# Zero matmuls in TensorE's ramp, two products on VectorE, GpSimd's share of e from unit 0 on, and another written-out order

## The chip, the cores and the metric

The kernel runs on one core of one Trainium2 chip. The metric is the device time of one execution in microseconds (us); five executions of the kernel before gave a median of 214.37 us (214.12 to 215.14). The engines are TensorE (PE, with its weight loads shown apart as PEld), VectorE (DVE), ScalarE (ACT), GpSimd (POOL) and SyncE (SP), whose queue issues nearly all DMAs.

## The reference

The input x and f_logit have 4 batches of 6336 tokens of 256 channels, in float32. A gated recurrence over the tokens is followed by a highway layer:

```python
sig = 1.0 / (1.0 + np.exp(-f_logit))
f = lower_bound + (1.0 - lower_bound) * sig
i = 1.0 - f
for t in range(S):
    h = f[:, t] * h + i[:, t] * x[:, t]
    y[:, t] = h
# then, on the y of all tokens
H = np.maximum(y @ w_h, 0.0)
T = 1.0 / (1.0 + np.exp(-(y @ w_t + b_t)))
out = T * H + (1.0 - T) * y
```

## The kernel before

The tokens are cut into 25 units. Units 0 to 23 are 1024 tokens of one batch each (8 blocks of 128), taken batch after batch, so a unit continues the recurrence of the unit four before it; unit 24 holds the last 192 tokens of all four batches, 8 blocks of 96. The first part of a unit's work (a "front") may be cut in pieces, by the table CUTS: unit 0 in 0a (blocks 0 and 1), 0b (2 and 3) and 0c (4 to 7), units 1, 2 and 24 in halves a and b. Fronts of other units are whole. The second part (a "back") is whole for units 0 to 23 and in halves for unit 24.

What is done with a piece, by the letters of the list PLAN (in what follows "S0c.1" is letter S for piece 0c, second channel half, and "Z0.1" the second half of letter Z of unit 0):

- L and X load f_logit and x (SP, line 106; five buffers each); Q loads the two weight matrices (line 125).
- U: u = sigmoid(-f_logit) on ACT (line 154). P: the product u*x, one instruction for every two blocks, on POOL (line 160, called from `gpsimd_mul`). Letter p is the same product on DVE (`vector_mul`, line 166), for those listed in EARLY; EARLY is empty.
- A: PE transposes u (line 198) and F: ACT makes f from it (line 205). B: PE transposes the product (line 215). S: DVE scans the recurrence from f and the transposed product (line 230).
- W: DVE prepares the weights (line 148), once.
- Z and G: PE multiplies y by the two weight matrices (line 245). T: ACT takes the sigmoid of Z (line 251). D: DVE makes d from y and G (line 256). E: DVE makes e = d*t (line 166). H: POOL makes the last 512 columns of e (line 160) where `shared(j)` is not 0, which is for units 3 to 23 here. O: PE adds y and e up, transposed back to tokens (lines 296 and 297), in two groups q of a back. C and V copy the result out of PSUM on ACT and DVE (line 303); V is there for the last three backs only. R stores it (SP, line 309).

PLAN is one string in which every letter is the next instruction group of its kind; the digit behind A, B, Z, G and O is the PSUM slot (0 to 2). Each engine works through its own letters strictly in this order (`pin`). So a wait at one letter holds up all later letters on the same engine. Slots for A and B (16-bit) and for Z, G and O (float32) are apart; a slot can be written again when its reader is done. When a POOL product or H follows DVE products or Es in the list, it also waits for those (`gpsimd_mul`, the list `port`).

Of the kernel before, what the change touches and what calls it, by code (L numbers as in the profile page):

```python
# [11 lines left out]
FP32 = mybir.dt.float32  # L12
BF16 = mybir.dt.bfloat16
# [6 lines left out]
def kernel(  # L20
# [16 lines left out]
    nc = tc.nc  # L37
    B, S, D = x.shape
    assert D == 256
    P = 128  # L40
    NH = D // P
    NB = 8
# [16 lines left out]
    fronts, backs = [], []  # L59
# [6 lines left out]

    LASTQ = 2

    EARLY = []

# [7 lines left out]
    singles = ctx.enter_context(tc.tile_pool(name="singles", bufs=1))  # L80
# [4 lines left out]
    def new(key, shape, dtype):  # L85
        return pools[key].tile([P, *shape], dtype, tag=key, name=key)

    def pin(ins):
        return tc.keep_in_program_order(ins)
# [12 lines left out]
    def load(i, name, src):  # L102
        u, j0, j1 = fronts[i]
        np_, j = units[u][0], run(fronts[i])
        t = fs[i][name] = new(name, [NB, D], FP32)
        pin(nc.sync.dma_start(t[:np_, :j1 - j0].rearrange("p (k j) d -> p k (j d)", j=j), tokens(src, u, j0, j1, j)))
# [6 lines left out]
    def shape(piece):  # L113

        u, j0, j1 = piece
        return units[u][0], j1 - j0

    lb = singles.tile([P, NH], FP32, name="lb")
    bt = singles.tile([P, NH], FP32, name="bt")
# [4 lines left out]
    def load_weights(k):  # L124
        pin(nc.sync.dma_start(w_raw[:, 1 - k], (moe_w_t, moe_w_h)[k].rearrange("(h p) o -> p h o", p=P)))
# [25 lines left out]
    def gate(i):  # L151
        np_, nb = shape(fronts[i])
        u = fs[i]["u"] = new("u", [NB, D], FP16)
        pin(nc.scalar.activation(u[:np_, :nb], fs[i]["lt"][:np_, :nb], AF.Sigmoid, scale=-1.0))  # L154
# [13 lines left out]
    def product(i, k, mul):  # L168
        np_, _ = shape(fronts[i])
        if "bv" not in fs[i]:  # L170
            fs[i]["bv"] = new("bv", [NB // 2, D, 2], BF16)
        mul(inner(fs[i]["bv"][:np_, k:k + 1])[:, 0], fs[i]["u"][:np_, 2 * k:2 * k + 2],
            fs[i]["xt"][:np_, 2 * k:2 * k + 2])

    def width(piece):
        np_, nb = shape(piece)
        return np_ * nb
# [5 lines left out]
    def psum(slot, shape, key, dtype):  # L183
        tag = ("one" if dtype in (FP16, BF16) else "two") + slot
        return ps1.tile([P, *shape], dtype, tag=tag, name=key)
# [73 lines left out]
    SHARE = 512  # L259

    def shared(j):

        return SHARE if width(backs[j]) == NB * P and j >= 3 else 0

    def e_cols(j, a, e):
        if "e" not in bs[j]:
# [3 lines left out]
    def e_dve(j):  # L270
        vector_mul(*e_cols(j, 0, width(backs[j]) - shared(j)))

    def e_pool(j):
        gpsimd_mul(*e_cols(j, width(backs[j]) - shared(j), width(backs[j])))
# [37 lines left out]
    def each(pieces, count):  # L312
        return [(i, k) for i, piece in enumerate(pieces) for k in range(count(piece))]

    def halves_of(pieces):
        return each(pieces, lambda p: len(halves(p)))
# [7 lines left out]
    kinds = {  # L324
        "L": (lambda i, _: load(i, "lt", f_logit), each(fronts, lambda p: 1)),
        "X": (lambda i, _: load(i, "xt", x), each(fronts, lambda p: 1)),
        "Q": (lambda i, k: load_weights(k), [(0, 0), (0, 1)]),
        "U": (lambda i, _: gate(i), each(fronts, lambda p: 1)),
        "P": (lambda i, k: product(i, k, gpsimd_mul), [p for p in products if p not in EARLY]),
        "p": (lambda i, k: product(i, k, vector_mul), [p for p in products if p in EARLY]),  # L330
        "A": (decay_pe, halves_of(fronts)),
        "F": (decay_act, each(fronts, lambda p: NH)),
# [6 lines left out]
        "D": (d_dve, each(backs, lambda p: NH)),  # L339
        "E": (lambda j, _: e_dve(j), each(backs, lambda p: 1)),  # L340
        "H": (lambda j, _: e_pool(j), [(j, 0) for j in range(len(backs)) if shared(j)]),
        "O": (o_pe, groups),
        "C": (lambda j, q: o_copy(j, q, nc.scalar.copy, 0, group(j, q)[2]), [p for p in groups if group(*p)[2]]),
# [3 lines left out]
    }  # L347

    PLAN = (
        "XLLLXXLXLQQUUA0A1PFFFUFUB0PSSB1A0FFPSSPB1A0XLLXLXXPFUFSSWWPB1A0G0Z1PFFUPSSDPXLLXLB0A1G2Z0PUTFFTPPB1S"  # L350
        "SDUSSEZ1A0G0G2A1DDPFTFFPPZ1A0B1O0O2PSSTFECCUB0Z1B1G0G2SDSDA0Z0TUFTPPPPPPA0G1B1FXLLLXRRXLXDESA0Z0Z2O1"
        "UFTCTB0G0A1O1O2SDPPPFCCB1A0Z1G0O2FTUCB0G1PPPHPSDSEDPA1Z0Z2B0O1FTUCTESA1G0G1B0DDHPPPPSZ2O0O1FUTCCB1SA"
        "0G2Z0B1FDUTPHPPSXXLRLRRRLRXLRRZ1A0G2O0PDTFCEEG1B1A0O2O0UFCCDSG1B0A1Z2Z0SDPHPPPPFTTA1B0O2O1G0HPSFCCZ2"
        "B1A0Z1DUTFTEG0O2PSPLXXRXRRRRDPPHCB1SA0O1G0Z2B1FCUTDEPSG1Z0A0O2FTCPDPPHB1A0Z1G0O2SFTCDEB0Z1A1G0PLLXRR"
        "RRSDPPPUFTO2B0A1Z0G1SHDCFTEO2B0G0Z1A1PPPPCUFTSDHO2B0A1G0Z1SCFTO2B0A1DEPSZ1G0PPPCUFTDHO2B0A1O0G1SCFCD"
        "EZ2B0A1Z0PSTFTPPPG1B1O2A0O0DUCFCSG1Z2A1B0HDELXLLRXRLLRXRRRRRXPSTFPPZ1G0O2B1DTCSZ1G2A0O0PHUFTCDEB1A0G"
        "2Z1O0PSPFTCDPPHB0G1G2A1Z0UFTSA0B1FDEDSPO1O0Z2B0PPCCTPHSO1A1G0Z2B0UFTCDEPSA1G0Z2O1PPDB0FTCSA1Z2G0O1PH"
        "FUCTDELXRRXXRRLRLXXRRRA1B0G0Z1PSFTO2DCB1A0G1Z0O2PPPHSUFCTDEB1A0Z1G2O0PSDFTCB0A1Z1G2SFPPPHDO0B1A0G2ET"
        "UCFPSO1PZ0CDTB1A0Z1G2SFTUHO0A0B1DFG1EPPPPSO2A0CCZ0DFB1O2Z1B0TCUTSESHPPG0A1Z2G1DDRRRRRRRRFFTA1B0O2Z0Z"
        "1FCFSEHTTG2B1G0O1RSDDCO2SRHCZ0G1STRO2TDDEZ0CTERTG1O2O0DVDVCO2CREVO1CRO0RCVRR"  # L360
    )
    assert all(PLAN.count(k) == len(places) for k, (_, places) in kinds.items())
    todo = {k: iter(places) for k, (_, places) in kinds.items()}
    letters = iter(PLAN)
    for k in letters:
        kinds[k][0](*next(todo[k]), *([next(letters)] if k in "ABZGO" else []))
# [1 line left out]
_INS = ['x', 'f_logit', 'lower_bound', 'moe_w_h', 'moe_w_t', 'moe_b_t']  # L368
# [26 lines left out]
```

## Time and profile before

| what | us |
|---|---|
| median of five executions | 214.37 |
| the profiled execution, whole | 214.27 |
| its span, first to last instruction | 212.5 |
| busy DVE / ACT / PE / POOL | 195.4 / 193.7 / 186.1 / 161.1 |
| first S (scan) starts | 9.53 |
| last V and last C end | 207.24, 207.38 |
| last store's issue ends | 208.45 |

The profile is read in this manner: a group is one line of the kernel, with the engine, what it writes and reads, the number of instructions, their busy time and the mean time of one. "Idle before" is the time in which the engine stood still ahead of these instructions, and who ended it. Instructions on one engine overlap a little, so the distance from start to start is shorter than the time of one: for ACT 1.80 us for U of a whole unit, 1.00 for an F or T of 1024 columns and 0.90 for a C; for DVE 2.26 for a scan of 1024 columns, 1.17 for a D, 0.58 for an E of 1024 elements.

### The profile page before, as it was taken

To read this page: it belongs to the slowest core of one execution; us is meant where nothing else is said; L and a number is where in the kernel's file an instruction comes from. 1 tells how busy PE (TensorE), PEld (TensorE's weight loads), DVE (VectorE), ACT (ScalarE), POOL (GpSimd) and SP (SyncE) were. 2 spreads that over 40 slices of the span, in tenths; PEclk is the share of its full clock that TensorE was granted. 3 is DMA by queue.
4 is the path that set the end of the run, shared out by engine and by line. 5 is a ranking of instruction groups with operands and counts; after the bars stand their busy time and mean duration, and the time that the engine had idled before them with its cause. 6 is when DMAs were issued, how large, how long until landed. Compare 5 with 4: busy or idle time off the path is not lost.

```text
span 212.5 us, 4591 instructions
## 1 busy us (share of the span) xinstructions
PE 186.1 (88%) x1775; PEld 131.5 (62%) x1800; DVE 195.4 (92%) x154; ACT 193.7 (91%) x194; POOL 161.1 (76%) x133
## 2 busy tenths in 40 slices
PE   0368988799898999999999999999999899999980
PEld 0255655567565767666767766668576676866770
DVE  1269999999999999999999999999999999999980
ACT  2757999999999999999999999999999999998750
POOL 4485745979599698978988998898898876866500
PEclk9999999999999999999999999999999999999996
DMA  4999999999999999999999999999999996252466
GB/s 97 401 410 430 424 427 427 424 419 426 425 419 426 420 423 421 425 430 410 427 418 423 432 423 418 426 413 431 416 428 405 352 405 266 86 214 99 195 250 201
DMA packets 17350, 78.69 MB, mean 370 GB/s; under 512 B 2352, under 2 KB 2864, under 8 KB 11952
## 3 DMA queue, kind: packets, MB, share of 16 engines
q1 hardware_dynamic: 16784, 78.39, 90.3%
q8 instruction: 14, 0.23, 0.4%
q10 hardware_dynamic: 544, 0.00, 0.1%
q14 instruction: 8, 0.07, 0.1%
HBM read 52.43 MB, written 25.95 MB: 369 GB/s over the span
## 4 chain that ended last, share of the span: by engine, by line
DMA 35%; PE 26%; ACT 19%; DVE 8%; issue 7%; POOL 1%; SPq 1%; ACTq 1%; DVEq 0%; POOLq 0%
DMA xt<-in_x_dram 12%; DMA lt<-in_f_logit_dram 12%; DMA out_dram<-o 12%; PE zp L245 7%; PE gp L245 6%; ACT t L251 5%; ACT o L303 5%; ACT u L154 5%; ACT f L205 5%; DVE d L256 4%; PE op L296 4%; PE op L297 3%; PE uT L198 3%; PE bT L215 3%; DVE y L230 3%
## 5 line engine op out<-in xcount | busy, mean ns | idle before, releaser
L160 POOL TENSOR_TENSOR bv<-u,xt 128x512 bf16<-128x512 f16 (+1 forms) x100 | 114.7, 1179 | 31.5 <-DVE e L166 11.0
L230 DVE TENSOR_TENSOR_SCAN y<-f,y,bT 128x1024 bf16<-128x1024 f16 (+3 forms) x56 | 106.4, 1918 | 2.3 <-PE bT L215 2.3
L205 ACT ACTIVATE f<-uT,ncc 128x1024 f16<-128x1024 f16 (+3 forms) x60 | 66.0, 1111 | 2.5 <-PE uT L198 2.5
L251 ACT ACTIVATE t<-zp,bt 128x1024 bf16<-128x1024 f32 (+1 forms) x52 | 63.8, 1249 | 0.7 <-PE zp L245 0.3
L256 DVE SCALAR_TENSOR_TENSOR d<-y,ncc,gp 128x1024 bf16<-128x1024 bf16 (+1 forms) x52 | 62.3, 1208 | 0.3 <-issue 0.2
L245 PEld LDWEIGHTS <-w_sb 128*128 128x128 f16 x400 | 38.0, 99 | 37.7 <-issue 5.9
L303 ACT COPY o<-op 128x1024 f32<-128x1024 f32 (+2 forms) x50 | 55.7, 1159 | 4.2 <-PE op L297 2.1
L154 ACT ACTIVATE u<-lt 128x2048 f16<-128x2048 f32 (+3 forms) x30 | 53.3, 1780 | 5.2 <-DMA lt<-in_f_logit_dram 5.2
L245 PE MATMUL gp<-y,w_sb 128*128 128x512 bf16 (+1 forms) x187 | 50.6, 382 | 1.6 <-ACT t L251 0.4
L245 PE MATMUL zp<-y,w_sb 128*128 128x512 bf16 (+1 forms) x188 | 49.6, 378 | 1.7 <-DVE d L256 0.6
L296 PE MATMUL op<-diag,y 128*128 128x128 f16 (+1 forms) x400 | 49.2, 219 | 1.9 <-ACT t L251 0.7
L160 POOL TENSOR_TENSOR e<-d,t 128x1024 bf16<-128x1024 bf16 x21 | 44.9, 2136 | 7.4 <-DVE e L166 2.6
L297 PE MATMUL op<-ident_b,e 128*128 128x128 bf16 (+1 forms) x400 | 49.2, 219 | 0.0
L297 PEld LDWEIGHTS <-e 128*128 128x128 bf16 (+1 forms) x400 | 44.7, 114 | 5.6 <-issue 3.4
L296 PEld LDWEIGHTS <-y 128*128 128x128 bf16 (+1 forms) x400 | 44.8, 114 | 2.7
L198 PE MATMUL uT<-ident_h,u 128*128 128x128 f16 (+1 forms) x400 | 32.1, 226 | 10.2 <-ACT u L154 7.4
L198 PEld LDWEIGHTS <-u 128*128 128x128 f16 (+1 forms) x400 | 27.3, 101 | 17.4 <-ACT u L154 7.6
L215 PE MATMUL bT<-ident_f,bv 128*128 128x128 f32 (+1 forms) x200 | 32.3, 284 | 5.0 <-DVE y L230 2.4
L215 PEld LDWEIGHTS bT<-ident_f,bv 128*128 128x128 f32 (+1 forms) x200 | 22.8, 145 | 11.5 <-issue 4.6
L166 DVE TENSOR_TENSOR e<-d,t 128x1024 bf16<-128x1024 bf16 (+2 forms) x26 | 18.9, 734 | 0.1
L230 DVE TENSOR_TENSOR_SCAN y<-f,bT 128x512 bf16<-128x512 f16 (+2 forms) x8 | 10.5, 1337 | 4.0 <-PE bT L215 4.0
L135 DVE TENSOR_SCALAR cc<-lb 128x2 f32<-128x2 f32 x1 | 0.2, 169 | 4.5 <-DMA lb<-in_lower_bound_dram 4.5
(19 smaller groups left out, 10.9 us busy)
## 6 DMA issues: line engine op xcount, KB each, us to landing
out_dram<-o SPq DMA_DIRECT2D x48, 512.0 KB, 13.6
lt<-in_f_logit_dram SPq DMA_DIRECT2D x21, 1024.0 KB, 14.7
xt<-in_x_dram SPq DMA_DIRECT2D x21, 1024.0 KB, 15.5
lt<-in_f_logit_dram SPq DMA_DIRECT2D x5, 512.0 KB, 8.1
xt<-in_x_dram SPq DMA_DIRECT2D x5, 512.0 KB, 8.2
lt<-in_f_logit_dram SPq DMA_DIRECT2D x2, 384.0 KB, 13.2
xt<-in_x_dram SPq DMA_DIRECT2D x2, 384.0 KB, 11.7
xt<-in_x_dram SPq DMA_DIRECT2D x2, 256.0 KB, 5.1
```

The lines of the kernel that those rows point to most:

```text
L154: pin(nc.scalar.activation(u[:np_, :nb], fs[i]["lt"][:np_, :nb], AF.Sigmoid, scale=-1.0))
L160: ins = pin(nc.gpsimd.tensor_mul(out_, a, b))
L198: pin(nc.tensor.transpose(uT[:, j * np_:(j + 1) * np_], fs[i]["u"][:np_, j, h * P:(h + 1) * P], ident_h[:np_, :np_]))
L205: pin(nc.scalar.activation(f[:, :N].rearrange("p (k q j) -> p k q j", q=np_, j=j), fs[i]["uT", h].rearrange("p (k j q) -> p k q j", q=np_, ...
L215: pin(nc.tensor.transpose(t[:, k // r, k % r], fs[i]["bv"][:np_, k, h * P:(h + 1) * P].rearrange("p d j -> p (d j)").bitcast(FP32), ident_ ...
L230: pin(nc.vector.tensor_tensor_scan(y, fs[i]["f", h][:, c:c + w], fs[i]["bT", h][:, c:c + w], 0.0 if prev is None else prev, op0=ALU.mult, ...
L245: pin(nc.tensor.matmul(p[:, a:e], w_sb[:, k, ki, h * P:(h + 1) * P], y_of(j)[:, ki, a:e], start=ki == 0, stop=ki == NH - 1))
L251: pin(nc.scalar.activation(bs[j]["t"][:, m, :width(backs[j])], bs[j]["zp", m], AF.Sigmoid, bias=bt[:, m:m + 1]))
L256: pin(nc.vector.scalar_tensor_tensor(bs[j]["d"][:, m, :width(backs[j])], y_of(j)[:, m], ncc[:, m:m + 1], bs[j]["gp", m], op0=ALU.mult, op1 ...
L296: pin(nc.tensor.matmul(o, y[:, h, cols], diag[:, h], start=True, stop=False))
L297: pin(nc.tensor.matmul(o, bs[j]["e"][:, h, cols], ident_b, start=False, stop=True))
L303: pin(copy(bs[j]["o", q][:np_, a:e], bs[j]["op", q][:np_, a:e]))
```

## The change

Four things are edited. EARLY names two products, (0, 0) and (2, 0): the product of piece 0a and the first of piece 0c are now letter p, on DVE. `shared` no longer asks for j >= 3, so units 0, 1 and 2 have an H on POOL too, and their E on DVE is 1024 elements long where it was 2048. A tile of zeros, `filler`, is set by DVE, and a new letter M is one matmul of it, 128x128 by 512 columns, into a PSUM tile `busy` that nobody reads; `busy` has the float32 slot 2, whose next user is Z0.0. And PLAN is another string, with 21 Ms in it.

```diff
-    EARLY = []
+    EARLY = [(0, 0), (2, 0)]
...
+    filler = singles.tile([P, 512], BF16, name="filler")
+    nc.vector.memset(filler, 0.0)
...
-        return SHARE if width(backs[j]) == NB * P and j >= 3 else 0
+        return SHARE if width(backs[j]) == NB * P else 0
...
-        "XLLLXXLXLQQUUA0A1PFFFUFUB0PSSB1A0FFPSSPB1A0XLLXLXXPFUFSSWWPB1A0G0Z1PFFUPSSDPXLLXLB0A1G2Z0PUTFFTPPB1S"
-        "SDUSSEZ1A0G0G2A1DDPFTFFPPZ1A0B1O0O2PSSTFECCUB0Z1B1G0G2SDSDA0Z0TUFTPPPPPPA0G1B1FXLLLXRRXLXDESA0Z0Z2O1"
...
-        "1FCFSEHTTG2B1G0O1RSDDCO2SRHCZ0G1STRO2TDDEZ0CTERTG1O2O0DVDVCO2CREVO1CRO0RCVRR"
+        "LLXXLXQQUUMMMMMMMMMA0pFFMMMMB1PSLXLXLXLSA0MMMMB1UFFpSSWWMMA0PFFUXLXLMMB1PSA0PSUFFUPPG0G1Z2B1DDSZ0STT"
+        "A0B1PPHEFFUPSXXLA0SPFFUO1B0O2LLXXA1PSSPCCFFUPG0G1B0PPPDSSDZ2Z0A1A0TTFFEZ2B1Z1A0TTUFG0G2SDDB1HPPPPHPO"
...
+        "DHFFO2G1B1TCPSRO0A0O2PCCFDSERG1G0RDSHZ2Z1B1DFTTSZ2G0O1HTTSDDCO2G1EERDO0CDO2CVRO1RCVZ0RCVTRTEO2O1CVRR"
...
+    busy = psum("2", [NB * P], "busy", FP32)
...
+        if k == "M":
+            pin(nc.tensor.matmul(busy[:, :512], filler[:, :P], filler, start=True, stop=True))
+            continue
```

Read by engine, the start of the two lists is this:

| engine | before | after |
|---|---|---|
| SP | X0a L0a L0b L0c X0b X0c L1a X1a L1b Q Q X1b L2a L2b X2a L3 X2b X3 | L0a L0b X0a X0b L0c X0c Q Q L1a X1a L1b X1b L2a X2a L2b X2b L3 X3 |
| PE | A0a A0b B0a B0b A0c B0c A1a B1a A1b G0.0 Z0.0 B1b A2a G0.1 Z0.1 B2a Z1.0 A2b | M x9, A0a, M x4, B0a A0b, M x4, B0b, M x2, A0c, M x2, B0c A1a G0.0 G0.1 Z0.0 B1a Z0.1 A1b B1b A2a O0.0 B2a O0.1 A2b |
| DVE | S0a S0b S0c W W S1a D0.0 S1b D0.1 S2a E0 D1.0 D1.1 S2b E1 S3.0 | p0a S0a p0c S0b W W S0c D0.0 D0.1 S1a E0 S1b S2a D1.0 S2b D1.1 E1 S3.0 |
| ACT | ... U2a U2b T0.0 F2a F2a T0.1 U3 F2b.0 T1.0 F2b.1 F3.0 T1.1 F3.1 C0 C0 U4 | ... U2a T0.0 T0.1 F1b F1b U2b F2a F2a U3 C0 C0 F2b F2b U4 T1.0 T1.1 F3.0 F3.1 |

The end of the two lists on PE and DVE, from G23.0 and D23.0 on:

| engine | before | after |
|---|---|---|
| PE | G23.0 B24b G23.1 O21.1 O22.0 Z24a G24a O22.1 Z24b G24b O23.0 O23.1 O24a O24b.0 O24b.1 | G23.0 G23.1 Z23.0 Z23.1 B24b Z24a G24a O22.0 O22.1 G24b O23.0 O23.1 O24a Z24b O24b.0 O24b.1 |
| DVE | D23.0 D23.1 S24b D24a D24a E23 E24a D24b.0 V23.0 D24b.1 V23.1 E24b V24a V24b | D23.0 S24a.1 D23.1 S24b D24a D24a E23 E24a D24b.0 D24b.1 V23.0 V23.1 V24a E24b V24b |

More of the change, by code (lines that the diff above doesn't have):

```diff
@@ L349 @@
     PLAN = (
-        "XLLLXXLXLQQUUA0A1PFFFUFUB0PSSB1A0FFPSSPB1A0XLLXLXXPFUFSSWWPB1A0G0Z1PFFUPSSDPXLLXLB0A1G2Z0PUTFFTPPB1S"
-        "SDUSSEZ1A0G0G2A1DDPFTFFPPZ1A0B1O0O2PSSTFECCUB0Z1B1G0G2SDSDA0Z0TUFTPPPPPPA0G1B1FXLLLXRRXLXDESA0Z0Z2O1"
-        "UFTCTB0G0A1O1O2SDPPPFCCB1A0Z1G0O2FTUCB0G1PPPHPSDSEDPA1Z0Z2B0O1FTUCTESA1G0G1B0DDHPPPPSZ2O0O1FUTCCB1SA"
-        "0G2Z0B1FDUTPHPPSXXLRLRRRLRXLRRZ1A0G2O0PDTFCEEG1B1A0O2O0UFCCDSG1B0A1Z2Z0SDPHPPPPFTTA1B0O2O1G0HPSFCCZ2"
-        "B1A0Z1DUTFTEG0O2PSPLXXRXRRRRDPPHCB1SA0O1G0Z2B1FCUTDEPSG1Z0A0O2FTCPDPPHB1A0Z1G0O2SFTCDEB0Z1A1G0PLLXRR"
@@ L355 @@
[L355 to L359, printed above, removed]
@@ L360 @@
-        "1FCFSEHTTG2B1G0O1RSDDCO2SRHCZ0G1STRO2TDDEZ0CTERTG1O2O0DVDVCO2CREVO1CRO0RCVRR"
+        "LLXXLXQQUUMMMMMMMMMA0pFFMMMMB1PSLXLXLXLSA0MMMMB1UFFpSSWWMMA0PFFUXLXLMMB1PSA0PSUFFUPPG0G1Z2B1DDSZ0STT"
+        "A0B1PPHEFFUPSXXLA0SPFFUO1B0O2LLXXA1PSSPCCFFUPG0G1B0PPPDSSDZ2Z0A1A0TTFFEZ2B1Z1A0TTUFG0G2SDDB1HPPPPHPO"
+        "1O0B0UCCSSZ2A1G1Z0B0EDTFTPPSPPPA1O2G1O0DHFUCCB1A0G1Z2Z0SFTTA1B0DEPSLLLXXRXRRLXRRRFUPG2O1B1O0A0DPPHCC"
+        "G2FSDZ1Z0A1B0G2EPSTTFUPO1O0B1DPPHCCA0G2Z1SFDZ0A1B0EPSTFTUPG2O1A1B0O0DPPHCCG2Z1FSDA0B1Z0EPRRRRXLLSTFT"
@@ new lines @@
+        "PO2G1B0O0DPUCCESZ1G2A1Z0TFDB0A1G1PHPSDTFUO2B1O0CCPPPHSA0G1Z2Z0B1DFTEPSA0G1O2TPFDPPHB0O0G1A1UCCFSXLRX"
+        "RRLRRRLLRXXDZ2Z0B0A1EPSTTFPO1G2B1A0O0DPPHCUCFSG1Z2Z0B1A0DEPSTTFPG1O2B0O0A1DPPHUCFCSG1Z2DA1B0Z0EPSG1P"
+        "TFTDPPHB1O2O0G1A0UCCSZ2B1Z0FTDEPXRXRRRLRSTPA0O1G2O0B1DPPHFCCSA0G1Z2Z0B1DUFTEPSA0G1O2TPFCO0B0A1G2DPPH"
+        "CSFUDZ1Z0A1B0G2EPSTTFPLLRRXLXRRXRRDPPHO1O0B1A0CCSFUG1Z2Z0A0B1DTTFEPSPG1O2O0B1A0DPPHCCFUSZ2G1A0B1Z0DE"
+        "PSTTFPG1O2O0B1A0DPPHCCFUSG2Z1B0Z0A1RLRRRRXLRXXLLDEPSTFTPG2O1B1O0A0DPPHCUCFSG2Z1B1Z0A0DTTFEPSG2O1B1O0"
@@ L361 @@
+        "A0PDPPHCUCFSG2Z1B1Z0A0TFTDEPSPG2O1B0A1G0UCFDPPHSDO2Z1B1A0Z0TFTCPSPG1B0A1EZ0O2FTCUDSG1A1Z0B0RRRRRXRRE"
+        "DHFFO2G1B1TCPSRO0A0O2PCCFDSERG1G0RDSHZ2Z1B1DFTTSZ2G0O1HTTSDDCO2G1EERDO0CDO2CVRO1RCVZ0RCVTRTEO2O1CVRR"
     )
+    assert set(PLAN) <= {*kinds, *"M012"}
     assert all(PLAN.count(k) == len(places) for k, (_, places) in kinds.items())
     todo = {k: iter(places) for k, (_, places) in kinds.items()}
+    busy = psum("2", [NB * P], "busy", FP32)
     letters = iter(PLAN)
     for k in letters:
+        if k == "M":
+            pin(nc.tensor.matmul(busy[:, :512], filler[:, :P], filler, start=True, stop=True))
+            continue
```

## The prediction

> **What bounds the kernel now.** I read the page first, then busy time in 5 us stretches, then the start times of single instructions.
>
> ```profile
> PE 186.1 (88%) x1775; PEld 131.5 (62%) x1800; DVE 195.4 (92%) x154; ACT 193.7 (91%) x194; POOL 161.1 (76%) x133
> ...
> DVE  1269999999999999999999999999999999999980
> ACT  2757999999999999999999999999999999998750
> ```
>
> DVE and ACT are both full in the middle and idle only at the two ends. By stretches (columns: length, then busy us and instructions of PE, PEld, DVE, ACT, POOL, then granted clock, DMA share, GB/s):
>
> ```profile
> 10.00:15.00 5.00, 3.64 (x22) 2.78 (x22) 3.17 (x5) 2.63 (x5) 4.67 (x5) 1.00 1.04 410
> 15.00:20.00 5.00, 3.39 (x16) 2.31 (x17) 5.00 (x6) 3.62 (x6) 3.12 (x3) 1.00 1.04 428
> 20.00:25.00 5.00, 4.78 (x31) 2.93 (x31) 4.96 (x5) 4.66 (x6) 2.92 (x3) 1.00 1.02 427
> 25.00:30.00 5.00, 4.44 (x37) 2.48 (x37) 5.00 (x5) 5.00 (x6) 2.30 (x3) 1.00 1.00 423
> ```
>
> DVE is full from 14 us on, ACT from 25. From there ACT has no idle time until 188 us. A whole unit costs ACT 1.80 (U) + 2x1.00 (F) + 2x1.00 (T) + 2x0.90 (C) = 7.6 us, and DVE 2x2.26 + 2x1.17 + 0.58 = 7.44. So DVE's lead in work is no use where the f of the next scan is late, and here it is nearly late: F14.0 and its scan S14.0 start 1.40 us apart, of which F itself takes 1.31.
>
> ```profile
> 116.78 1.31 ACT L205 ACTIVATE f<-uT,ncc 128x1024 f16<-128x1024 f16 x1
> ...
> 118.18 2.34 DVE L230 TENSOR_TENSOR_SCAN y<-f,y,bT 128x1024 bf16<-128x1024 f16 x1
> ```
>
> **So the time is ACT's work, plus what ACT loses in the ramp, plus the tail behind the last scans.** The change does not alter ACT's work. I therefore ask when ACT ends U3 (27.06 us before; the letters that it has done by then are the same in both lists), and how long the tail is.
>
> **The clock.** The granted-clock column says 1.00 throughout the ramp, but durations say otherwise:
>
> ```profile
> 18.34 1.91 PE L245 MATMUL gp<-y,w_sb 128*128 128x512 bf16 x4
> ...
> 22.32 1.03 PE L245 MATMUL gp<-y,w_sb 128*128 128x512 bf16 x4
> ```
>
> The same four matmuls take 1.91 and 1.03 us (0.43 and 0.215 each): PE runs at half speed until about 21.1. The end shows what takes the clock away:
>
> ```profile
> 205.43:208.84 3.41, 1.08 (x19) 0.93 (x16) 1.37 (x2) 1.21 (x3) 0.00 (x0) 1.00 1.00 369
> 208.84:212.40 3.56, 0.00 (x0) 0.00 (x0) 0.00 (x0) 0.00 (x0) 0.00 (x0) 0.50 0.45 148
> ```
>
> It falls to 0.50 at 208.84, 2.3 us after the last matmul (206.5), with 1.08 us of PE work in the 3.4 us before.
>
> **The change, part by part.**
>
> *Edits at no cost.* The filler's memset meets a DVE that waits until 4.49; the first nine M (9x0.43 = 3.9 us from about 1.3) a PE that waits until 6.73 for U0a. Without that cover they would cost 0.3 and 3.9 us. Slot 2 has no other user before Z0.0. In work: DVE gains 3x0.53 on E0 to E2 (1.21 to 0.68) and pays two products. No DVE row shows a product of these types. [...] Above, 1.19, the row W: 512 elements, two float32 inputs from SBUF. [...] POOL pays 3x2.14 - 2x1.18 = 4.1 us; it is idle for 51 us.
>
> [...] No run here shows a product on DVE.
>
> *Loads.* Queue order sets landings: before, bytes land at some 512 KB in 1.25 us (423 GB/s), X0c at about 10.5, L1a at 11.7. With X0a third, it lands when the third 256 KB did (7.3, where U0b waited for L0b). X0c stays at 10.5; the two Q move ahead of L1a and make it 13.0. L3 moves from the place of 7168 KB to 7680 KB: 24.3 instead of about 23.2, before ACT asks for it. Stores move on SP too: R0.0 now stands behind X9, and lands near 60; C4.0, which needs its buffer, comes near 67. Hidden; without that cover, some 2 us.
>
> *The ramp's chain with PE at full speed.* p0a 7.3 to 8.0; B0a and S0a end at 9.9. p0c waits for X0c: 10.5 to 11.2. Behind it on DVE stand S0b and W, and on POOL the second product of 0c waits for it by `port`. S0b (1.3), W (2.3) and S0c (2.4) follow without a gap and end at 17.15, where before S0c ended at 16.46 and W at 18.68. G0.0 ends 0.5 us later, G0.1 and Z0.0 0.86 each, B1a 0.45, Z0.1 0.86: T0.1 starts at 20.9 (before 24.25, but with three Fs ahead of it). Then T 1.0, F1b 1.1, U2b 1.0, F2a 1.1 and U3 1.8 bring ACT to 26.9: **0.2 us ahead of before**. D0.0 comes at 17.8; counting DVE's letters on from there, S3.0 could start at 33.8 instead of 34.94. But ACT must now do C0 (1.8), U4 (1.8) and T1.1 (1.0) ahead of F3.0: 29.20 + 4.6 - 0.2 = 33.6, ended at 34.7, and B3.0 has F3.0's PSUM slot and comes after it: S3.0 at 35.2. F4.1 has 4.6 us more ahead of it (40.59 to 45.0), ending at 46.2; S4.1 started at 46.26. DVE's gain is gone by unit 4. Later, U23 and C18.1 stand ahead of F21.1 (171.27 + 2.7 - 0.2 = 173.8; with F's 1.45 there, S21.1 at 175.25 instead of 174.78). I take 0.3 us late into the tail, between -0.4 and +0.9.
>
> *Does the clock hold?* Between the last M (11.3) and the first G0.0 (15.8 half, 17.05 the rest) PE has B0c and A1a, 0.9 us in 4.5. That is less than the share with which it fell at 208.84. So I expect half speed again at G0.0. Before, the clock came 2.8 us after the first 512-wide matmul; 2.8 us at half speed lose 1.4 us, in just the chain to T0.1: **+1.4** (0 if the clock holds; 2.9 if it comes only behind Z0.1).
>
> [...]
>
> *The tail.* Before, Z24b stood ahead of O23.0. Now it stands behind O24a and waits for slot 0 besides (O23.0, read by V23.0). From the end of E23: three O at 0.89, Z24b 0.65 + 0.17 latency, two T 1.07, E24b 0.55, two half O 0.9 and V 0.69 with some 0.35 of hand-overs: 7.05 us. Before, E23's end at 201.84 to V's end at 207.24 are 5.4.
>
> ```profile
> 202.07 1.05 ACT L251 ACTIVATE t<-zp,bt 128x384 bf16<-128x384 f32 x2 [0.33 <-DVE e L166]
> ...
> 204.87 0.55 DVE L166 TENSOR_TENSOR e<-d,t 128x768 bf16<-128x768 bf16 x1
> ```
>
> The sigmoids that stood at 202.07, beside other work, now stand at the end of the chain. The last V comes 1.6 us later. Of that, 0.9 comes back: before, the last store queued 0.6 us behind two others, and now it has fewer bytes ahead. **+0.7** (0 to 1.5).
>
> **Sum.** 214.27 (the profiled execution, 0.1 under the median) + 0.3 + 1.4 + 0.7 = 216.7 us.
>
> **Rivals.**
>
> 1. *The clock holds* through the gap: 214.27 + 0.3 + 0.7 = 215.3 (214.3 to 216.2). For it: nine plus twelve Ms make PE denser than it ever was there. Against it: the row at 208.84.
> 2. *Faster: ACT is not what decides.* Place: F3.0 and F4.1. If T0.1 comes 1.5 us sooner than I count (ACT at U3's end 1.7 ahead), all of DVE's gain passes: 1.1 at S3.0 and 0.5 for E2, and the 0.42 us that DVE waited for a transpose at 76.4: 214.27 - 2.0 + 0.7 = 213.0; 212.6 with no loss in the tail. It decides when S4.1 starts below 45.5. For it: DVE has 10.3 us of idle time before 14 us, and the list for units 5 to 20 leaves F 0.5 us or more of room. Against it: ACT has no idle time to give between 25 and 188 us.
> 3. *Nothing is left over:* the front gains what the tail loses, 214.3; also what comes out if PE's clock does not matter to ACT at all.
>
> **Chances.** Forecast (clock falls back) 0.45; rival 1 0.17, of which 0.05 within 0.3%; rival 2 0.26; rival 3 0.12. A difference of 0.3% (0.64 us) is about what a measurement of this kernel can tell from none. So faster 0.26, same 0.17, slower 0.57. The range takes rival 2 down to 212.8 and the forecast with p at 1.19 and a later clock up to 218.2; some 2 in 10 lie outside. The forecast's own range is 215.3 to 218.2.
>
> **What would show it.** The G0.0 group of four 512-wide matmuls: 1.0 us if the clock holds, above 1.5 if it fell. T0.1's start: 20.9 or 22.3. U3's end: 26.9 or 28.3. S4.1 against 46.26. E23's end to the last V's end: 7.05 against 5.4. p's duration: 0.69 to 1.19. I am wrong if DVE's scans of units 3 and 4 do not wait for F, or if the last sigmoids are not on the chain.

## The result and the profile after

The changed kernel takes **214.87 us** (median of 24 executions, 214.66 to 216.19; the kernel before beside it 214.31): ratio **1.0029, 95% interval 1.0019 to 1.0038**. Slower, by 0.3% where 1.1% was forecast. The profiled execution took 214.82 us, its span is 213.0: 0.55 us over the 214.27 of before.

The page of the kernel after, as far as it answers to that of before:

```profile
PE 190.3 (89%) x1794; PEld 131.8 (62%) x1821; DVE 196.4 (92%) x157; ACT 194.4 (91%) x194; POOL 165.0 (77%) x134
...
DVE  2599796999999999999999999999999999999971
ACT  4569979999999999999999999999999999996851
```

DVE starts working earlier (2, 5 in its first two slices for 1, 2). But it now has holes, the 7 and the 6 in its fifth and seventh slices. The stretches show it in numbers (columns as before):

```profile
10.00:15.00 5.00, 3.14 (x26) 1.74 (x26) 5.00 (x7) 2.64 (x5) 2.37 (x3) 1.00 1.05 421
15.00:20.00 5.00, 3.89 (x26) 2.17 (x24) 4.53 (x5) 4.76 (x6) 4.58 (x5) 1.00 1.03 421
20.00:25.00 5.00, 2.73 (x35) 2.43 (x36) 4.07 (x4) 5.00 (x7) 5.00 (x4) 1.00 1.02 428
25.00:30.00 5.00, 4.95 (x44) 3.25 (x43) 4.86 (x5) 3.66 (x6) 3.36 (x4) 1.00 1.02 428
```

DVE is busy 5.00 of 5 us from 10 to 15 us (3.17 before), and loses 0.47 and 0.93 us in the next two stretches, where before it lost next to none (5.00 and 4.96).

**The clock held.** PE's four matmuls of a weight group take 1.03 us at 16.69, not 1.91:

```profile
15.62 1.24 PE L249 MATMUL gp<-y,w_sb 128*128 128x512 bf16 x5 [0.58 <-DVE y L234]
16.69 1.03 PE L249 MATMUL zp<-y,w_sb 128*128 128x512 bf16 x4
```

**Where the ramp's gain went.** DVE's timeline after, from the second early product to S3.0 (start, duration, and in brackets the idle time before with what ended it):

```profile
9.90 0.74 DVE L170 TENSOR_TENSOR bv<-u,xt 128x512 bf16<-128x512 f16 x1 [0.58 <-DMA xt<-in_x_dram]
...
11.81 1.39 DVE L152 SCALAR_TENSOR_TENSOR w_sb<-o,cc 128x512 f16<-128x512 f32 x2
...
16.03 2.47 DVE L260 SCALAR_TENSOR_TENSOR d<-y,ncc,gp 128x1024 bf16<-128x1024 bf16 x2 [0.47 <-PE gp L249]
...
20.66 0.96 DVE L170 TENSOR_TENSOR e<-d,t 128x1024 bf16<-128x1024 bf16 x1
...
25.14 2.33 DVE L234 TENSOR_TENSOR_SCAN y<-f,bT 128x512 bf16<-128x512 f16 x2 [1.08 <-PE bT L219]
...
33.83 1.39 DVE L170 TENSOR_TENSOR e<-d,t 128x1024 bf16<-128x1024 bf16 x1 [1.57 <-ACT t L255]
35.68 2.29 DVE L234 TENSOR_TENSOR_SCAN y<-f,bT 128x1024 bf16<-128x1024 f16 x1 [0.46 <-PE bT L219]
```

S2a waits 1.08 us because O0.0 stands ahead of B2a on PE and waits for H0 until 23.6. E1 waits 1.57 us for T1.1, which ACT does only after U4, and ACT stands idle ahead of U4 for its load:

```profile
27.25 1.28 ACT L209 ACTIVATE f<-uT,ncc 128x512 f16<-128x512 f16 x2
29.88 1.91 ACT L158 ACTIVATE u<-lt 128x2048 f16<-128x2048 f32 x1 [1.34 <-POOL bv L164]
31.69 2.10 ACT L255 ACTIVATE t<-zp,bt 128x1024 bf16<-128x1024 f32 x2
33.69 2.12 ACT L209 ACTIVATE f<-uT,ncc 128x1024 f16<-128x1024 f16 x2
```

The row names a GpSimd product, which ended at 29.81; the load itself landed at 29.79 (issued at 14.94, 14.85 us in the queue). U4 needs the load, not the product.

So the account from DVE's first scan to S3.0, by starts in the three profiles ("old list, filled" is the kernel before with nothing but the matmuls on zeros, run below):

| us | before | after | old list, filled |
|---|---|---|---|
| first scan starts | 9.53 | 8.05 | 9.06 |
| DVE idle from there to S3.0 | 1.83 | 4.16 | 1.39 |
| the two W | 2.30 | 1.39 | 1.39 |
| S3.0 starts | 34.94 | 35.68 | 33.07 |
| S4.1 starts | 46.26 | 46.94 | 44.74 |
| E23 starts | 201.26 | 201.79 | 199.98 |

After starts 1.48 us sooner and has 0.91 less of W, loses 2.33 more in waits and 0.62 in the second early product, which makes 0.56; it is 0.74 late at S3.0, the rest lying in small changes of length. From there to the tail DVE has no hole longer than 0.12 us, and the lateness is carried along: 0.68 at S4.1, 0.53 at E23.

**The tail.** DVE and ACT at the end, after:

```profile
207.16 0.56 DVE L170 TENSOR_TENSOR e<-d,t 128x768 bf16<-128x768 bf16 x1 [0.48 <-ACT t L255]
208.86 0.69 DVE L307 COPY o<-op 96x512 f32<-96x512 f32 x1 [1.13 <-PE op L301]
```

```profile
206.08 1.05 ACT L255 ACTIVATE t<-zp,bt 128x384 bf16<-128x384 f32 x2
```

The last sigmoids do stand on the chain (206.08, against 202.07 before), and E24b comes 2.3 us later. From E23's end to the last V's end it is 7.07 us, against 5.29. But from there to the span's end it is 3.50 us, against 5.25. The two differences cancel.

### The profile page after: what moved, and what is told of

Its sections match the earlier page's. It is cut to its first block, busy times and chain, and to the rows that moved or that the text cites. A ratio compares the mean times of both kernels' runs of the same rounds, so it can differ in the third digit from the quotient of the medians.

```text
span 213.0 us, 4618 instructions
## 1 busy us (share of the span) xinstructions
PE 190.3 (89%) x1794; PEld 131.8 (62%) x1821; DVE 196.4 (92%) x157; ACT 194.4 (91%) x194; POOL 165.0 (77%) x134
## 4 chain that ended last, share of the span: by engine, by line
PE 41%; ACT 28%; DMA 13%; DVE 10%; issue 5%; POOL 1%; SPq 1%; ACTq 0%; DVEq 0%; POOLq 0%
DMA lt<-in_f_logit_dram 11%; PE gp L249 10%; PE zp L249 9%; ACT f L209 9%; ACT t L255 8%; ACT u L158 7%; PE op L300 6%; PE op L301 6%; DVE y L234 5%; PE bT L219 5%; PE uT L202 5%; ACT o L307 4%; DVE d L260 3%; DMA xt<-in_x_dram 2%; POOL e L164 1%
## 5 line engine op out<-in xcount | busy, mean ns | idle before, releaser
L164 POOL TENSOR_TENSOR bv<-u,xt 128x512 bf16<-128x512 f16 (+1 forms) x98 | 112.1, 1176 | 26.9 <-DVE e L170 9.6
L209 ACT ACTIVATE f<-uT,ncc 128x1024 f16<-128x1024 f16 (+3 forms) x60 | 67.5, 1144 | 0.7 <-PE uT L202 0.7
L255 ACT ACTIVATE t<-zp,bt 128x1024 bf16<-128x1024 f32 (+1 forms) x52 | 61.3, 1279 | 1.3 <-PE zp L249 0.8
L164 POOL TENSOR_TENSOR e<-d,t 128x1024 bf16<-128x1024 bf16 x24 | 51.6, 2151 | 8.7 <-DVE e L170 7.4
L307 ACT COPY o<-op 128x1024 f32<-128x1024 f32 (+2 forms) x50 | 54.1, 1188 | 4.4 <-PE op L301 4.4
L249 PE MATMUL gp<-y,w_sb 128*128 128x512 bf16 (+1 forms) x177 | 48.0, 376 | 2.5 <-DVE y L234 0.9
L219 PE MATMUL bT<-ident_f,bv 128*128 128x128 f32 (+1 forms) x200 | 30.9, 276 | 6.0 <-DVE y L234 2.9
L202 PE MATMUL uT<-ident_h,u 128*128 128x128 f16 (+1 forms) x400 | 30.7, 219 | 2.6 <-ACT f L209 1.1
L170 DVE TENSOR_TENSOR e<-d,t 128x1024 bf16<-128x1024 bf16 (+1 forms) x26 | 18.8, 728 | 2.2 <-ACT t L255 2.1
L234 DVE TENSOR_TENSOR_SCAN y<-f,bT 128x512 bf16<-128x512 f16 (+2 forms) x8 | 10.5, 1342 | 2.1 <-PE bT L219 2.1
L373 PE MATMUL busy<-filler 128*128 128x512 bf16 x21 | 8.0, 531 | 1.2 <-DVE filler L120 1.2
```

The costliest lines, as they stand in the source:

```text
L164: ins = pin(nc.gpsimd.tensor_mul(out_, a, b))
L202: pin(nc.tensor.transpose(uT[:, j * np_:(j + 1) * np_], fs[i]["u"][:np_, j, h * P:(h + 1) * P], ident_h[:np_, :np_]))
L209: pin(nc.scalar.activation(f[:, :N].rearrange("p (k q j) -> p k q j", q=np_, j=j), fs[i]["uT", h].rearrange("p (k j q) -> p k q j", q=np_, ...
L219: pin(nc.tensor.transpose(t[:, k // r, k % r], fs[i]["bv"][:np_, k, h * P:(h + 1) * P].rearrange("p d j -> p (d j)").bitcast(FP32), ident_ ...
L234: pin(nc.vector.tensor_tensor_scan(y, fs[i]["f", h][:, c:c + w], fs[i]["bT", h][:, c:c + w], 0.0 if prev is None else prev, op0=ALU.mult, ...
L249: pin(nc.tensor.matmul(p[:, a:e], w_sb[:, k, ki, h * P:(h + 1) * P], y_of(j)[:, ki, a:e], start=ki == 0, stop=ki == NH - 1))
```

## The experiments

Each kernel was timed in five rounds beside the kernel before. All compute the reference's output in full. "To E23" is the start of E23 in the profile, less that of the kernel after (201.79).

| kernel | median us | range | ratio to before, interval | S4.1 less after's | to E23 |
|---|---|---|---|---|---|
| before | 214.31 | 213.69 to 215.32 | 1 | -0.68 | -0.53 |
| after | 214.87 | 214.66 to 216.19 | 1.0029 [1.0019, 1.0038] | 0 | 0 |
| no_fill | 215.42 | 214.69 to 216.30 | 1.0046 [1.0025, 1.0066] | +1.42 | +1.46 |
| no_share | 215.07 | 214.84 to 216.65 | 1.0046 [1.0021, 1.0072] | | |
| no_early | 214.96 | 214.84 to 215.50 | 1.0028 [1.0010, 1.0047] | +0.08 | +0.10 |
| l4_first | 215.72 | 215.52 to 216.41 | 1.0060 [1.0037, 1.0084] | +0.72 | +0.92 |
| old_tail | 214.95 | 214.77 to 216.26 | 1.0040 [1.0022, 1.0059] | -0.10 | -0.17 |
| t1_first | 216.58 | 215.16 to 218.15 | 1.0116 [1.0077, 1.0155] | +1.59 | +1.78 |
| t1_tail | 217.07 | 215.49 to 219.03 | 1.0115 [1.0077, 1.0153] | +2.29 | +2.50 |
| before_fill | 213.48 | 212.79 to 214.92 | 0.9962 [0.9941, 0.9984] | -2.20 | -1.81 |
| bf_share | 215.87 | 215.59 to 216.32 | 1.0069 [1.0046, 1.0092] | +0.26 | +0.81 |
| bf_share12 | 213.63 | 213.03 to 214.94 | 0.9971 [0.9949, 0.9993] | -2.13 | -1.53 |
| bf_fill2 | 213.10 | 212.84 to 213.77 | 0.9941 [0.9919, 0.9964] | -1.56 | -1.58 |
| bf_best | 213.39 | 213.04 to 214.55 | 0.9962 [0.9945, 0.9979] | -1.77 | -1.17 |

The last two columns say the same thing twelve times: what a kernel has lost or won by unit 4, it has lost or won, to within 0.6 us, at E23. They are of one profiled execution each, which need not be the median one: no_fill's took 216.30 us, before_fill's 213.00. The one profile of no_share is of an execution of 248.04 us and is not read.

### One part of the change undone

**no_fill**: the 21 Ms taken out of the new list.

```diff
-LLXXLXQQUUMMMMMMMMMA0pFFMMMMB1PSLXLXLXLSA0MMMMB1UFFpSSWWMMA0PFFUXLXLMMB1PS
+LLXXLXQQUUA0pFFB1PSLXLXLXLSA0B1UFFpSSWWA0PFFUXLXLB1PS
```

> The changed kernel without its 21 M. In its profile the clock rose at 7.0 us and T0.1 started at 19.4. Without M the clock should rise some 3 us behind the first G0.0 matmul (14.45), so T0.1 comes about 1.5 us later and U3 ends near 27 instead of 25.5. Theory 1 (ACT's order decides, and ACT then waits 1.34 us for the load L4 at 28.5 to 29.9): U4 absorbs nearly all of it, 214.9 to 215.3 us. Theory of the prediction (every us that ACT loses ahead of U3 comes out at the end): 216.2 to 216.5.

Measured: 215.42, 0.1 above the first range. The clock rises at 18.78 only, S3.0 is at 37.12 (35.68) in its profile, an execution of 216.30 us. By the medians the Ms are worth about half a microsecond in the new list, but the two intervals overlap, so this is not settled.

**no_share**: GpSimd's share of e from unit 3 on only, as before; the first three H leave the list.

```diff
-        return SHARE if width(backs[j]) == NB * P else 0
+        return SHARE if width(backs[j]) == NB * P and j >= 3 else 0
```

> The changed kernel with shared() asking for j >= 3 again and the first three H taken out of the list. In the changed kernel E0, E1, E2 (1024 elements) took 0.96, 1.39 and 1.14 us beside POOL's work, before (2048 elements) 1.20, 1.23 and 1.21; so DVE's work moves by 0.1 us only. Theory 1 (ACT's order decides): 214.7 to 215.0. Rival (GpSimd's share slows DVE where it matters, in the front): E0 to E2 cost the same but D, S and O of units 0 to 2 come earlier, 214.2 to 214.5.

Measured: 215.07. No gain and no clear loss: in the new list's order the share is not what costs.

**no_early**: no product on DVE.

```diff
-    EARLY = [(0, 0), (2, 0)]
+    EARLY = []
```

> The changed kernel with EARLY empty: both p are P on POOL, in the same places of the list. DVE has 1.46 us less work; the first scan comes some 0.8 us later (POOL takes 1.18 instead of 0.73), U3 ends up to 1 us later. Theory 1 (ACT's order decides, the wait for L4 absorbs it): 214.7 to 215.1. Rival (DVE's work decides, 1.07 us more of it in the changed kernel): 213.4 to 214.0.

Measured: 214.96, the same as with them. The two products bring the first scan forward (8.05 for 8.84) and bring the end nothing.

**old_tail**: the last forty letters in the old order.

```diff
-CO2G1EERDO0CDO2CVRO1RCVZ0RCVTRTEO2O1CVRR
+CO2Z1G0EERCTTDO2VDO1RVCO0CRREVCO2RO1CVRR
```

> The changed kernel with the last 40 letters in the order that the kernel before has: Z24b and G24b ahead of O23, T24b ahead of C23, V ahead of C. Theory 1 (the new order of the tail is neutral: in the changed kernel's profile E23's start to the end of the last V takes 7.76 against 5.98 us, but the last V to the span's end 3.45 against 5.27, because the stores no longer queue): last V about 1.8 earlier, the stores' queue back, time within 0.3 of 214.87. Theory 2 (the prediction's third step, which charged the tail with +0.7): 214.2.

Measured: 214.95; the last V ends at 207.99 (209.54 after) and the span is 213.0 in both. Theory 1 holds: no gain or loss by the tail's new order shows, and the prediction's third term was not there.

### Is it the load of unit 4?

**l4_first**: L4 and X3 change places in the load queue.

```diff
-FFUXLXLMMB1P
+FFUXLLXMMB1P
```

> The changed kernel with the loads L4 and X3 exchanged in SP's queue, nothing else. L4 lands some 2.5 us earlier, so ACT's 1.34 us of waiting ahead of U4 goes; X3 lands 2.5 us later, and POOL's products of unit 3 end near 34.5, about when B3.0 gets its PSUM slot from F3.0. Theory 1 (ACT's order decides): U4 to F3 come 1.3 us earlier, S4.1 near 45.7 instead of 46.94, and the end 0.5 to 1.0 us earlier, 213.9 to 214.4. Rival (DVE's own work decides from unit 5 on): S4.1 earlier but the end within 0.2 of 214.87.

Measured: 215.72, which neither theory had. U4 no longer waits for its load, but X3 comes later, and GpSimd stands idle 4.07 us for it. So H2 comes later and still runs when E2 starts, and E2 takes 2.11 us, where it took 1.14 in the kernel after:

```profile
30.08 7.23 POOL L164 TENSOR_TENSOR bv<-u,xt 128x512 bf16<-128x512 f16 x6 [4.07 <-DMA xt<-in_x_dram]
...
43.87 2.13 POOL L164 TENSOR_TENSOR e<-d,t 128x1024 bf16<-128x1024 bf16 x1
```

```profile
44.43 2.11 DVE L170 TENSOR_TENSOR e<-d,t 128x1024 bf16<-128x1024 bf16 x1
```

The DMA engines are full here (share 1.02 to 1.05 in the stretches above), and the wait moved from one load to the other: the products of unit 3 start at 30.08, in the kernel after at 27.52. In this profile the clock was at 0.50 from 23.50 to 26.91 as well, which in the kernel after it was not, and S2a waited 2.13 us for 1.08. That fall alone does not explain the time: 3.41 us at 0.50 take 0.008 off the mean granted clock of an execution, and the one with 0.994 took 215.52 us.

**t1_first**: U4 and the first two products of unit 4 behind T1.0, T1.1 and F3.0. **t1_tail**: that and old_tail's end.

```diff
-PCCFFUPG0G1B0PPPDSSDZ2Z0A1A0TTFFE
+PCCFFPG0G1B0PDSSDZ2Z0A1A0TTFUPPFE
```

> The changed kernel with the letters of U4 and of its first two products moved behind T1.0, T1.1 and F3.0, so that ScalarE does not stand idle 1.34 us at U4 for the load of unit 4 while T1 is ready. Theory 1 (VectorE's place at unit 4 is what the end inherits, and U4's wait for its load is what made E1 late): Z1.0 ends near 29.4, so T1.1 ends near 31.7 instead of 33.8, E1 starts at 32.3 instead of 33.8, S3.0 at 33.0 to 34.2 (35.7), S4.1 at 45.3 to 45.8 (46.9), and the time falls by 1.1 to 1.6, to 213.3 to 213.8. Theory 2 (ScalarE's total work, not this wait, sets S4.1, as the prediction has it): ScalarE loses the 1.34 us no less, because it waits for something else; S4.1 within 0.4 of 46.9 and 214.6 to 215.1.

> Both edits: U4 behind T1.0, T1.1 and F3.0, and the tail in the order of the kernel before. Theory 1 (tail neutral, U4's wait decides): as U4's move alone, 213.3 to 213.8. Theory 2 (the tail cost 0.7 as the prediction has it): 0.7 under U4's move alone.

Measured: 216.58 and 217.07, where theory 1 had 213.3 to 213.8: it fell. In t1_first's profile ACT waits 1.29 us, now for Z1.0, and S2a waits 2.13 us, with the clock at 0.50 from 23.14 to 26.55; E1 then waits 0.10 us only, and S3.0 starts 0.83 us sooner than in the kernel after. But F3.1 behind U4 makes G2.0, and D2.0 with it, late, and E2 takes 2.12 us beside H2:

```profile
26.33 2.33 DVE L234 TENSOR_TENSOR_SCAN y<-f,bT 128x512 bf16<-128x512 f16 x2 [2.13 <-PE bT L219]
...
38.40 2.47 DVE L260 SCALAR_TENSOR_TENSOR d<-y,ncc,gp 128x1024 bf16<-128x1024 bf16 x2 [1.26 <-PE gp L249]
```

```profile
30.85 2.12 ACT L255 ACTIVATE t<-zp,bt 128x1024 bf16<-128x1024 f32 x2 [1.29 <-PE zp L249]
```

Theory 2 had it right that ACT loses the time in any case, but put no price on the rest. The fall of the clock alone does not explain it here either: the execution of t1_tail with a mean granted clock of 0.997, which leaves no room for it, took 215.49 us, still more than after. So taking away the wait at U4 in this manner gained nothing, and t1_tail shows no gain from the old tail.

### The fill alone, in the old list

**before_fill**: the kernel before, with the zeros' tile and 22 Ms between its letters (the edit has 9, 2, 3, 2 and 6; the expectations count 21 here and in bf_share, and 24 in bf_fill2, each one too few).

```diff
-XLLLXXLXLQQUUA0A1PFFFUFUB0PSSB1A0FFPSSPB1A0XLLXLXXPFUFSSWWPB1A0G0Z1
+XLLLXXLXLQQUUMMMMMMMMMA0A1MMPFFFUFUB0MMMPSSB1A0MMFFPSSPB1A0MMMMMMXLLXLXXPFUFSSWWPB1A0G0Z1
```

> The kernel before with nothing but the zeros' tile and the 21 matmuls on it put between its letters in the ramp. Theory 1 (the clock alone brings little here: VectorE has W, D0 and E0 in its list's order and reaches unit 4 by its own work, U3 a little earlier): U3 up to 1.5 earlier, S4.1 0 to 0.5 earlier, 213.8 to 214.4. Theory 2 (ScalarE's ramp loss goes straight to the end, as the prediction's bound has it): U3 1.5 or more earlier, S4.1 and the end 1.0 to 1.5 earlier, 212.9 to 213.4.

Measured: **213.48, 0.38% faster than before** (0.16 to 0.59%). Median and S4.1 (1.52 earlier) stand with theory 2 or beside it. But the way is DVE's, as this profile shows:

```profile
9.06 1.26 DVE L233 TENSOR_TENSOR_SCAN y<-f,bT 128x256 bf16<-128x256 f16 x2 [3.57 <-PE bT L218]
10.81 1.39 DVE L233 TENSOR_TENSOR_SCAN y<-f,y,bT 128x256 bf16<-128x256 f16 x2 [0.48 <-PE bT L218]
13.11 2.45 DVE L233 TENSOR_TENSOR_SCAN y<-f,y,bT 128x512 bf16<-128x512 f16 x2 [0.91 <-PE bT L218]
15.47 1.39 DVE L151 SCALAR_TENSOR_TENSOR w_sb<-o,cc 128x512 f16<-128x512 f32 x2
```

After 13.11 DVE has no idle time at all down to S3.0, which is 1.87 us sooner than before: 0.47 from the first scan, 0.44 from shorter waits, 0.91 from W (0.05 is left over). The W part is not the clock's doing; the last section tells whose. By the medians 0.83 us of this is left at the end. So the Ms by themselves are good, and the other list costs 1.4 us with the fill (214.87 less 213.48) and 1.1 without it (215.42 less 214.31).

**bf_share**: before_fill, and GpSimd's share of e from unit 0 on, an H behind each of E0, E1 and E2 (the first is shown).

```diff
-        return SHARE if width(backs[j]) == NB * P and j >= 3 else 0
+        return SHARE if width(backs[j]) == NB * P and j >= 0 else 0
...
-SDUSSEZ1A0G0
+SDUSSEHZ1A0G0
...
```

> The kernel before with the 21 matmuls on zeros, and GpSimd's share of e in the first three backs too, each H right behind its E in the list: the part of the other list that its name tells, in the old order. Against the same without the share (213.48; S3.0 at 33.07, S4.1 at 44.74). Theory 1 (a place on GpSimd decides): H0 at 26.7 to 28.8 stands ahead of the products of unit 3, which begin 1.3 us later (28.8 for 27.5) and end at 33.4; S3.0 at 34.0 to 34.3, 1 us late, of which the shorter E0 to E2 (3 x 0.53) give back part: S4.1 and the end 0 to +0.7, 213.5 to 214.2. Theory 2 (the prediction's sum, 0.53 saved per back with the GpSimd beside it): end 1.6 earlier, 211.9.

Measured: 215.87, 2.4 over before_fill. Theory 1's direction, three times its size. GpSimd and DVE:

```profile
27.18 2.13 POOL L163 TENSOR_TENSOR e<-d,t 128x1024 bf16<-128x1024 bf16 x1 [0.86 <-DVE e L169]
29.26 5.00 POOL L163 TENSOR_TENSOR bv<-u,xt 128x512 bf16<-128x512 f16 x4
34.22 2.12 POOL L163 TENSOR_TENSOR e<-d,t 128x1024 bf16<-128x1024 bf16 x1
```

```profile
31.80 1.44 DVE L169 TENSOR_TENSOR e<-d,t 128x1024 bf16<-128x1024 bf16 x1
34.68 2.29 DVE L233 TENSOR_TENSOR_SCAN y<-f,bT 128x1024 bf16<-128x1024 f16 x1 [1.45 <-PE bT L218]
38.58 1.28 DVE L259 SCALAR_TENSOR_TENSOR d<-y,ncc,gp 128x1024 bf16<-128x1024 bf16 x1 [1.61 <-POOL bv L163]
```

H0 pushes the products of unit 3 back to 29.26 (28.8 was counted). Not counted: E1, halved, now runs beside a product and takes 1.44 us, more than the whole E1 in before_fill (1.22); and H1 pushes the products of unit 4. Nor was the clock: PE waits for the late products, has 1.29 us of work from 31.54 to 34.95, and is at 0.50 from there to 38.37, so the matmuls of G2.0 and G2.1 take 2.78 us for 1.89 in before_fill. The D in the last row is D2.0, which waits for G2.0; the product that the row names is not among what it reads. An execution whose mean granted clock of 0.994 leaves no room for such a fall took 215.75 us all the same.

**bf_share12**: the share from unit 1 on. **bf_fill2**: before_fill with three more Ms, between A0a and A0b. **bf_best**: both.

```diff
-... and j >= 3 else 0
+... and j >= 1 else 0
```

```diff
-UUMMMMMMMMMA0A1MMPFFF
+UUMMMMMMMMMA0MMMA1MMPFFF
```

> As the one above, but with the share from the second back on, whose H1 falls into the 2.63 us in which GpSimd stands idle (32.07 to 34.70) and H2 behind E2. Theory 1 (a place on GpSimd decides, and VectorE's work is the bound from unit 1 on): E1 and E2 0.5 shorter each, S3.0 at 32.5, S4.1 at 43.6 to 44.2, the end 0.5 to 1.1 earlier than 213.48: 212.4 to 213.0. Theory 2 (something else than VectorE's work sets S4.1): within 0.2 of 213.48.

> The kernel before with 24 matmuls on zeros: three more, between the decay transposes of 0a and those of 0b, in the window from 4.88 to 8.29 after which the clock fell to 0.5 until 11.71 with 21 of them. Theory 1 (the clock follows the work in such a window): the clock holds from 4.9 on, the transposes between 8.3 and 11.7 take half as long, S0c starts 0.3 to 0.8 earlier (13.11), and the end as much: 212.7 to 213.2. Theory 2 (S0c waits for loads and products, not for the clock): within 0.2 of 213.48.

> Both of the two edits above: the share from the second back on, and the three further matmuls on zeros. If both theories 1 hold, the sum of their gains: 211.7 to 212.7; if neither, 213.3 to 213.7.

Measured: 213.63, 213.10 and 213.39, with intervals that overlap each other's and before_fill's. The share gains nothing: H1 found its gap and E1 shrank to 0.70, but E2 took 1.37 beside a product. As to the Ms, bf_fill2's own profile shows the clock at 0.5 from 7.26 to 10.67 all the same, and in bf_best's, where it holds from 5.07 on, S0c starts at 13.25 (before_fill 13.11): S0c does not wait for the clock there. For the share theory 2 holds. For the Ms the 213.10 lies in theory 1's range, but what theory 1 asks for did not come: the clock fell, and S0c started at 13.46. All four kernels with the fill and without H0 beat before and after; which of them is best is not settled by these runs.

## Why the prediction was wrong

- **The clock term (+1.4) failed.** The step was that "PE has B0c and A1a, 0.9 us in 4.5" between the last M and G0.0, "less than the share with which it fell at 208.84". The fall does not go by the share of work in the gap. In all 13 profiles the clock changes at distances that are multiples of 3.41 us, so the trace is cut into windows of that length from the first rise. In the kernel after the windows round the gap have 1.94 and 2.48 us of PE work, since each catches Ms or weight matmuls at one side, and the one at 20.65 has 1.80 (PE's busy time is the first number after the length):

```profile
10.41:13.83 3.42, 1.94 (x21) 1.24 (x21) 3.42 (x6) 2.32 (x3) 1.20 (x2) 1.00 1.04 424
13.83:17.24 3.41, 2.48 (x15) 1.17 (x14) 2.94 (x4) 2.21 (x3) 3.26 (x3) 1.00 1.03 420
...
20.65:24.07 3.42, 1.80 (x22) 1.50 (x23) 3.42 (x4) 3.42 (x6) 3.42 (x3) 1.00 1.00 422
```

  Transposes count in this work: without A and B the window at 10.41 has 0.59 us of PE work and the clock held, while in before_fill it fell after a window with 0.77 us besides transposes (from 4.88; 1.40 with them). In all six profiles that have the Ms at these places the clock held through the gap; it fell later in four of them, between 23.14 and 24.48, with the windows lying elsewhere in each. In no_early the window that has 1.80 above has 1.42, and the clock falls in the next window:

```profile
20.63:24.05 3.42, 1.42 (x16) 1.18 (x17) 3.21 (x4) 3.42 (x7) 3.42 (x3) 1.00 1.01 429
24.05:27.46 3.41, 3.41 (x29) 3.35 (x30) 1.50 (x2) 2.71 (x3) 2.25 (x3) 0.50 1.01 423
```

- **T0.1 and U3 were 1.5 us earlier still than the sum had them with the clock held** (19.37 for 20.9; ACT is through with U3 at 25.46 for 26.9). The sizes that were off: X0c landed at 9.77 for 10.5, and W was counted at 2.3 and took 1.39 (before, its two instructions took 0.73 and 1.66; why is told at the end). The 0.69 counted for the product p was the author's estimate: it is the length of the copy V in before (203.14, 0.69 us), and no run shows that a product takes as long. The two p took 0.73 and 0.74, and not the 1.19 of the row W, which was a mean of the two.
- **+0.3 for the order of ACT and F came out at 0.53, in part by luck.** Its places are met: F3.0 at 33.69 (33.6), F4.1's end at 46.26 (46.2), S21.1 at 175.35 (175.25); S3.0 at 35.68 (35.2). But S4.1 did not wait for F4.1: DVE had work without a hole from S3.0 on and reached S4.1 at 46.94 only. And the 1.5 us that ACT had in hand at U3 went in the 1.34 us at U4, whose load the prediction did not price: it followed L3's place in the queue and stopped there.
- **The E's saved 0.15 us in all, not 3 x 0.53.** E0 to E2 took 0.96, 1.39 and 1.14 (1.20, 1.23 and 1.21 at twice the length).
- **The tail (+0.7) failed by the part given back.** The chain was counted at 7.05 and measured at 7.07; from the last V to the span's end 1.75 us came back, not 0.9. The last store is issued 0.03 us behind the last V instead of 0.64 (0.6 was counted), lands 2.40 us after that instead of 3.08 (0.3 was counted), and the span ends 1.07 us after the landing instead of 1.53, which was not counted and is not the tail's order, since old_tail has 1.07 too. With the old tail in the new list the two parts are 5.68 and 5.00 us, nearly the same sum as 7.07 and 3.50.
- **What bounds the kernel.** "The time is ACT's work" held at unit 3 only, where S3.0 waits 0.46 us behind F3.0. ACT has no idle time from unit 4 to 180 us either, but DVE does not wait for it: F14.0 now ends 1.8 us before its scan, where the prediction's row had it nearly late, and nothing came of that; the longest later wait that a row puts down to an F is 0.10 us, at S21.1.

```profile
114.64 1.49 ACT L209 ACTIVATE f<-uT,ncc 128x1024 f16<-128x1024 f16 x1
```

(S14.0 starts at 117.97.) Rival 1, the clock holding, was nearest with 215.3 and had its condition right; but its sum keeps the tail's 0.7, which was not there. Rival 2's condition, T0.1 1.5 us sooner, came true without its effect.

What stays open is which step of the new order costs its 1.4 us. The three waits of 3.1 us in all are shown; taking away the one at U4, by the load or by the letter's place, brought each time other losses (S2a's 2.13 us, E2's 2.11 and 2.12, D2.0's 1.26). O0 behind B2a was not tried.

## What to carry to other kernels

Filling TensorE's ramp with matmuls on zeros was worth 0.4% here (before_fill, 213.48 us), where DVE, the engine that is full afterwards, started sooner (9.06 for 9.53) and went on without a hole from 13.11 to S3.0: try it alone, in the old order. Follow an early gain to the first place where the full engine waits again, and price each load that is asked for sooner, not only the first. A share moved to GpSimd saved DVE 0.15 us in 3.64 here (E0 to E2), because the half that stayed ran beside another GpSimd product.

## What the runs showed of the hardware

**An E or a W that ran beside a GpSimd instruction ended 0.54 or 0.55 us after it.** An E or a W reads two operands from SBUF. In the profiles of before and after each E of 1024 columns that started 0.15 us or more ahead of the end of a running GpSimd product or H ended 0.54 or 0.55 us after that end, whatever its start; one that started later took its usual 0.66 to 0.69 us. The second W of before, which started 1.11 us ahead, did the same, and so did E2 of l4_first and E1 of bf_share. Some of them:

| instruction | starts | GpSimd product ends | it ends |
|---|---|---|---|
| second W, before | 17.02 | 18.13 | 18.68 |
| E0, after | 20.66 | 21.08 | 21.63 |
| E1, after | 33.83 | 34.67 | 35.22 |
| E2, after | 44.68 | 45.29 | 45.83 |
| E2, l4_first (H2 for the product) | 44.43 | 46.00 | 46.54 |
| E1, bf_share | 31.80 | 32.69 | 33.24 |

And a GpSimd instruction that starts while such an E or W runs is stretched: H0 of after took 2.58 us instead of 2.13, the product that starts 1.06 us into the second W of before 1.62 instead of 1.18, and the last product of unit 3 in bf_share as long. (In one case, bf_fill2 at 26.3 us, the two started 0.03 us apart, and the product, recorded as the first, was the one stretched.) The scans and D, which read one operand from PSUM, show nothing of it: in before and after all 96 Ds of 1024 columns took 1.25 to 1.28 us, and all 84 scans of 1024 columns 2.27 to 2.35. That is why W is 0.91 us shorter in after and before_fill: in before a product started 0.07 us ahead of the second W (16.95 and 17.02), in before_fill one started behind it and was itself stretched, and in after none ran beside it for more than 0.12 us.

**The clock fell after each window with 1.45 us of PE work or less, and after none with 1.77 or more.** Of all windows of 3.41 us at full clock in the 13 profiles, those with up to 1.45 us of PE work, transposes counted, were each followed by a fall, those from 1.77 us up by none, and between 1.57 and 1.73 there were both. So a window need not be empty: five of those that were followed by a fall in the first 25 us have 1.40 to 1.45 us. The first rise lies anywhere from 3.85 to 7.00 us with the Ms early in the list, in one execution (bf_share12) at 12.80.
